# Splitting the softmax numerators into two tiles, each with its own DMA transposition

## The chip, the cores and the metric

The kernel runs on one core of a Trainium2 chip. The metric is the device time of one execution in microseconds. Beside it stands a profile of one execution, with the start and length of every instruction on every engine.

## The reference

Attention over pooled queries, then two feed-forward layers:

```python
q_pool = q.reshape(B, H, S // 2, 2, D).mean(axis=3)      # B 4, H 8, S 1152, D 64
scores = q_pool @ k.T / sqrt(D)                          # 576 x 1152 for each head
attn   = softmax(scores);  x = attn @ v                  # x: 2304 tokens x 512
h = x @ w_in;   x = (h * cos(h)) @ w_out                 # d_ff 2048
h = x @ w_in2;  out = (h * sigmoid(h)) @ w_out2
```

Everything is float32. The kernel gets near that accuracy with 16-bit matmuls: each operand is cut into a high half (rounded to float16) and a low half (the remainder, also float16), and the products high x high, low x high and high x low are summed.

## The kernel before

**Attention.** Heads are taken in 16 pairs (4 batches of 4). A pair gives 9 query tiles of 128 rows, 144 tiles in all. One tile goes through these steps:

- scores on TensorE (PE) into `sp`, line 391 (line 399 for the ninth tile of a pair, whose two halves belong to two heads);
- VectorE (DVE) scales them into `sc` and takes the maximum (line 410, two pieces; `nb` from line 415);
- ScalarE (ACT) makes the exponential in place (line 418), then writes the high numerators as float16 into the first half of `hl` (line 424, `tile_hi`);
- GpSimd (POOL) subtracts, which gives the low numerators in the second half of `hl` (line 429, `tile_lo`);
- one DMA transposition on SyncE's queue (SP, line 431) turns all of `hl`, 128 rows of 2304 numbers, into `hlT`, 18 blocks of 128 x 128;
- PE weighs V with it (`tile_pv`): for each of 9 blocks `c` a matmul with the high block against high and low V (130 columns, line 442) and one with the low block against high V (65 columns, line 446), into `pv`.

The tiles `sc`, `hl` and `hlT` have 4 buffers each. The weighing of a tile is written 4 tiles behind its scores (`LAG`).

**Around it.** Beside the attention of batches 1 to 3, PE, ACT, DVE and POOL work on the first feed-forward layer of finished batches (lines 522 to 594). Its input blocks `xn` take a buffer of `hl` and are transposed by line 508, 16 blocks of 128 x 128 in one DMA. The first layer's weights are decoded during batch 0 (lines 206 to 240), the second layer's during and after batch 3. The second layer comes last (PE lines 522 and 603).

**Order.** All DMAs of the kernel are issued by SP, in one queue: loads of q, k, v and weights (lines 177, 293 to 302), transpositions of q and k (`qT`, `kT`, lines 357 and 367, 18 blocks each) and of the numerators. The order on every engine is fixed when the program is built, by priorities and by the builder's own estimate of times; on the chip each engine runs its list strictly in that order.

Of the kernel before, what the change touches and what calls it, by code (L numbers as in the profile page):

```python
# [12 lines left out]
F16 = mybir.dt.float16  # L13
I32 = mybir.dt.int32
AF = mybir.ActivationFunctionType
ALU = mybir.AluOpType
# [11 lines left out]
NB_N, NB_SC, NB_H, NB_T, NB_S = 2, 4, 4, 4, 5  # L28
# [16 lines left out]
def attention_moe_moe_kernel(ctx, tc, q, k, v, w_in1, w_out1, w_in2, w_out2, out):  # L45
# [3 lines left out]
    nc = tc.nc  # L49
    B, H, S, D = q.shape  # L50
    SQ = S // 2
    DM, DFF = w_in1.shape
    NC = DM // 128
    NF = DFF // 128
    KC = S // 128
# [22 lines left out]
    def scale_steps(m, pool, res, top, wide=False):  # L78

        n = m.shape[1]
        if wide:
            w = small.tile([128, 1], F32, name="mw", tag="mw")
            wi, mi = w.bitcast(I32), m.bitcast(I32)
            nc.vector.tensor_scalar(
                out=wi, in0=mi, scalar1=3, scalar2=0x3F800000, op0=ALU.logical_shift_left, op1=ALU.bitwise_and
            )
            nc.vector.scalar_tensor_tensor(  # L90
                out=wi, in0=mi, scalar=1 << 30, in1=wi, op0=ALU.bitwise_and, op1=ALU.bitwise_or
            )
            m = w
        bc = pool.tile([128, 2, GW], F32, tag="h", name="bm")[:, 0, 0:4]
        nc.tensor.matmul(bc[:, 0:n], mean, m, start=True, stop=True)
        yield
        s, u = res
        nc.vector.tensor_scalar(
            out=u, in0=bc[:, 0:n], scalar1=TINY, scalar2=2.0**(9 - top), op0=ALU.max, op1=ALU.mult
        )  # L100

        nc.vector.tensor_scalar(
            out=s.bitcast(I32), in0=u.bitcast(I32), scalar1=EXP_MASK, scalar2=EXP_MASK,
            op0=ALU.bitwise_and, op1=ALU.bitwise_xor,
        )
        nc.vector.tensor_scalar(
            out=u.bitcast(I32), in0=u.bitcast(I32), scalar1=EXP_MASK, scalar2=None, op0=ALU.bitwise_and
        )

    def absmax(out_, in_, axis=AX.X):  # L110
        nc.vector.tensor_reduce(out=out_, in_=in_, axis=axis, op=ALU.max, apply_absolute_value=True)
# [9 lines left out]
    def early(g, n):  # L121
        while True:
            with ahead(n):
                r = next(g, END)
            if r is END:
                return
            yield r
# [139 lines left out]
    def att_pools(stack):  # L267
        at = Weights()
        at.p = stack.enter_context(tc.tile_pool(name="att", bufs=2, side="right", reuse_waits="tile"))
        at.src_stack = ExitStack()  # L270
        at.src = at.src_stack.enter_context(tc.tile_pool(name="src", bufs=2, side="right", reuse_waits="tile"))
        at.ps_s = stack.enter_context(tc.tile_pool(name="ps_s", bufs=1, space=PSUM, side="right"))
        at.ps_v = stack.enter_context(tc.tile_pool(name="ps_v", bufs=1, space=PSUM, side="right"))
        return at
# [103 lines left out]
    def tile_scores(at, P, t):  # L378


        T = Pair()
        T.P, T.t = P, t

        parts = [(0, 512), (512, S)]
        T.sp = [(a, z, at.ps_s.tile([128, z - a], F32, tag="sp%d" % a, name="sp")) for a, z in parts]
        if t < 2 * NT:
            kT = P.kT[t // NT]
            for a, z, sp in T.sp:
                for o, n in segs:
                    for e in range(2 if a <= o < z else 0):  # L390
                        nc.tensor.matmul(  # L391
                            sp[:, o - a:o - a + n], P.qT[e][:, t, :], kT[:, o:o + n], start=(e == 0), stop=(e == 1)
                        )
        else:
            for a, z, sp in T.sp:
                for o, n in segs:
                    for e in range(2 if a <= o < z else 0):
                        for i in range(2):
                            nc.tensor.matmul(
                                sp[i * 64:(i + 1) * 64, o - a:o - a + n], P.qT[e][:, t, i * 64:(i + 1) * 64],  # L400
                                P.kT[i][:, o:o + n], start=(e == 0), stop=(e == 1),
                            )
        return T
# [14 lines left out]
        nc.scalar.activation(out=T.sc, in_=T.sc, func=AF.Exp, scale=-1.0, bias=nb)  # L418

    def tile_hi(at, T, on_act):  # L420
        T.hl = at.p.tile([128, 2, S], F16, tag="hl", name="hl", bufs=NB_H)
        hi = T.hl[:, 0, :]
        if on_act:
            nc.scalar.activation(out=hi, in_=T.sc, func=AF.Copy)  # L424
        else:
            nc.vector.tensor_copy(hi, T.sc)

    def tile_lo(at, T):
        nc.gpsimd.tensor_tensor(out=T.hl[:, 1, :], in0=T.sc, in1=T.hl[:, 0, :], op=ALU.subtract)  # L429
        T.hlT = at.p.tile([128, 2, KC, 128], F16, tag="hlT", name="hlT", bufs=NB_T)  # L430
        nc.sync.dma_start_transpose(
            out=T.hlT.rearrange("p e c k -> p (e c) k"), in_=T.hl.rearrange("p e s -> p (e s)")
        )

    def tile_pv(at, T):
        P, t, G = T.P, T.t, T.G
        if T.gi == 0:
            G.pv = at.ps_v.tile([128, GT, 2, D + 1], F32, tag="pv", name="pv")
        hs = [(slice(0, 128), t // NT)] if t < 2 * NT else [(slice(0, 64), 0), (slice(64, 128), 1)]
        for r, i in hs:  # L440
            for c in range(KC):
                nc.tensor.matmul(  # L442
                    G.pv[r, T.gi], T.hlT[:, 0, c, r], P.vt[i][:, c],
                    start=(c == 0), stop=(c == KC - 1), skip_group_check=True,
                )
                nc.tensor.matmul(  # L446
                    G.pv[r, T.gi, 0], T.hlT[:, 1, c, r], P.vt[i][:, c, 0],
                    start=False, stop=(c == KC - 1), skip_group_check=True,
                )

# [25 lines left out]
    def x_scale_consts(w, s, u, first):  # L476


        c = Weights()
        uo = w.uoT if first else w.uo  # L480
        c.k = small.tile([128, 1], F32, tag="ck", name="ck", bufs=3)
        c.a = small.tile([128, w.npc], F32, tag="ca%d" % w.npc, name="ca", bufs=3)
        c.y = small.tile([128, uo.shape[1]], F32, tag="cy%d" % first, name="cy", bufs=3)
        two_pi = 2.0 * math.pi
        nc.vector.tensor_scalar(
            out=c.k, in0=s, scalar1=w.kg, scalar2=two_pi if first else 1.0, op0=ALU.mult, op1=ALU.mult
        )
        nc.vector.tensor_scalar(
            out=c.a, in0=w.ui, scalar1=u, scalar2=0.25 / two_pi if first else 0.25, op0=ALU.mult, op1=ALU.mult
        )  # L490
        nc.vector.tensor_scalar(out=c.y, in0=uo, scalar1=u, scalar2=w.ug, op0=ALU.mult, op1=ALU.mult)
        return c

    def x_split(at, mp, x32, i, blk, w):

        m = small.tile([128, 1], F32, name="xm", tag="xm")
        absmax(m, x32, AX.XY)
        yield
        s = small.tile([128, 1], F32, name="xs", tag="xs")
        u = small.tile([128, 1], F32, name="xu", tag="xu")  # L500
        yield from early(scale_steps(m, ps_h, (s, u), 14), P_CH)
        blk.c = x_scale_consts(w, s, u, True)
        xn = at.p.tile([128, 2, 2, DM], F16, tag="hl", name="xn", bufs=NB_H)
        nc.scalar.activation(out=xn[:, 0], in_=x32, func=AF.Copy, scale=s)
        nc.vector.scalar_tensor_tensor(out=xn[:, 1], in0=x32, scalar=s, in1=xn[:, 0], op0=ALU.mult, op1=ALU.subtract)
        yield
        blk.T = mp.p.tile([128, 2, 2, NC, 128], F16, tag="x%d" % i, name="xT", bufs=1)
        nc.sync.dma_start_transpose(
            out=blk.T.rearrange("p e t c k -> p (e t c) k"), in_=xn.rearrange("p e t d -> p (e t d)")
        )  # L510
        blk.xh = lambda c: blk.T[:, 0, :, c, :]
        blk.xl = lambda c: blk.T[:, 1, :, c, :]

# [106 lines left out]
    if True:  # L620
# [6 lines left out]
        at = att_pools(att_stack)  # L627
# [67 lines left out]
        P = {}  # L695
# [23 lines left out]
        x32 = {}  # L719
# [27 lines left out]
        def drain_pv():  # L747
            T = inflight.pop(0)
            G = T.G
            with ahead(P_PV):  # L750
                tile_pv(at, T)
# [35 lines left out]
        for n, (b, j) in enumerate(pairs):  # L787
# [7 lines left out]
            for o in range(0, len(seq), GT):  # L795
                G = Pair()
# [9 lines left out]
            for idx, (G, gi, t) in enumerate(order):  # L806
                with ahead(P_SC):
                    T = tile_scores(at, P[n], t)
# [40 lines left out]
        for i in range(2):  # L849
            T = wpool.tile([128, B, 2, 128], F16, tag="x32_%d" % i, name="xrT")  # L850
# [68 lines left out]
        for n in range(NB):  # L919
            nyb = y_load(n + 1) if n + 1 < NB else None  # L920
            gen = y_split(nyb) if nyb else None
            for f in range(NF):
# [7 lines left out]
                if len(pend) > 8:  # L930
                    blk, ff, nn = pend.pop(0)
# [43 lines left out]
```

## Time and profile before

| | |
|---|---|
| time, median of 3 runs | 1414.32 us (1410.59 to 1415.83) |
| profiled execution, first to last instruction | 1411.7 us |
| mean granted TensorE clock | 0.928 of full speed |
| busy: PE, DVE, ACT, POOL | 82%, 70%, 54%, 40% of the span |

The profiled execution's span of 1411.7 us is within the spread of the three timed runs, 2.6 us below their median; nothing else is recorded around it. The attention lasts from the start to about 860 us. From there to about 1008 us the rest of the first layer runs beside the decoding of the second layer's weights, and from 1008 us to the end the second layer, with PE all but always busy. The busy shares are averages over these stages, so each stage is read by itself.

### The profile page before, as it was taken

How to read it: one execution, taken by the hardware profiler on the slowest of the kernel's cores; microseconds unless marked ns; L12 is line 12 of the kernel's file. 1: busy time of each engine (PE TensorE's matmuls, PEld its weight loads, DVE VectorE, ACT ScalarE, POOL GpSimd, SP SyncE). 2: the span in 40 equal slices, each digit the busy share in tenths (PEclk: the TensorE clock that was granted, in tenths of full speed). 3: DMA queues.
4: the chain of work that ended last, by engine and by line, in shares of the span. 5: the costliest groups of instructions: out<-in, count | busy, mean ns of one | idle time of the engine just before them, and what ended most of it. 6: DMA issues, size and time to landing. Idle time of an engine off the chain costs nothing. (4 is left out here: it accounts for less than half of the span.)

```text
span 1411.7 us, 24909 instructions
## 1 busy us (share of the span) xinstructions
PE 1164.1 (82%) x10020; PEld 853.2 (60%) x10020; DVE 988.5 (70%) x1848; ACT 768.7 (54%) x907; POOL 568.2 (40%) x296
## 2 busy tenths in 40 slices
PE   1465356787897768898889889978899999999998
PEld 0243233475675556666667678867776666666664
DVE  7999997678678888977999985999933322223221
ACT  3686487668777678777788785555421111111110
POOL 1577276535656466646666563553600000000000
PEclk9966568799999899999999999989999999999999
DMA  7799789987799999989999964544110000000001
GB/s 232 190 238 213 186 157 206 202 167 137 149 194 171 198 205 205 176 156 185 156 208 182 220 131 86 147 120 129 52 60 31 31 6 25 31 31 16 16 2 29
DMA packets 493075, 186.17 MB, mean 132 GB/s; under 512 B 433056, under 2 KB 467872, under 8 KB 492960
## 3 DMA queue, kind: packets, MB, share of 16 engines
q1 hardware_dynamic: 492960, 184.59, 61.9%
q8 instruction: 78, 1.28, 0.4%
q14 instruction: 37, 0.30, 0.1%
HBM read 66.58 MB, written 9.44 MB: 54 GB/s over the span
## 5 line engine op out<-in xcount | busy, mean ns | idle before, releaser
L429 POOL TENSOR_TENSOR hl<-sc,hl 128x1152 f16<-128x1152 f32 x144 | 368.7, 2569 | 194.0 <-ACT hl L424 109.8
L391 PE MATMUL sp<-kT,qT 128*128 128x512 f16 (+1 forms) x768 | 196.2, 373 | 112.0 <-DVE sc L410 85.9
L535 ACT ACTIVATE hk<-h,ca 128x512 f32<-128x512 f32 x144 | 97.9, 682 | 318.0 <-PE h L522 318.0
L522 PEld LDWEIGHTS <-ih 128*128 128x128 f16 x2304 | 227.3, 100 | 66.9 <-issue 7.3
L410 DVE TENSOR_SCALAR_CACHE_REDUCE sc<-sp,psu 128x512 f32<-128x512 f32 (+1 forms) x288 | 229.0, 807 | 48.1 <-PE sp L391 46.8
L418 ACT ACTIVATE sc<-sc,nb 128x1152 f32<-128x1152 f32 x144 | 179.9, 1250 | 91.0 <-DVE nb L415 78.2
L442 PE MATMUL pv<-vt,hlT 128*128 128x130 f16 (+1 forms) x1440 | 196.1, 238 | 37.4 <-DMA hlT<-hl 29.6
L522 PE MATMUL h<-ys,ih 128*128 128x256 f16 x1152 | 196.2, 273 | 1.0 <-ACT hk L535 1.0
L522 PE MATMUL h<-xT,ih 128*128 128x256 f16 x1024 | 190.6, 280 | 2.1 <-ACT hk L535 1.3
L442 PEld LDWEIGHTS <-hlT 128*128 128x128 f16 (+1 forms) x1440 | 148.0, 111 | 67.3 <-DMA hlT<-hl 39.5
L446 PE MATMUL pv<-vt,hlT 128*128 128x65 f16 (+1 forms) x1440 | 188.4, 208 | 0.0
L391 PEld LDWEIGHTS <-qT 128*128 128x128 f16 x768 | 78.0, 110 | 180.0 <-issue 138.5
L424 ACT ACTIVATE hl<-sc 128x1152 f16<-128x1152 f32 x144 | 165.3, 1155 | 23.4 <-DMA hlT<-hl 12.2
L570 DVE TENSOR_SCALAR gh<-hk,ck 128x1024 f16<-128x1024 f32 x36 | 27.0, 751 | 206.2 <-PE o L603 198.6
L582 PE MATMUL y<-gl,oh 128*128 128x256 f16 x576 | 158.4, 275 | 2.9 <-POOL gl L563 2.9
L582 PE MATMUL y<-gh,oh 128*128 128x256 f16 x576 | 158.4, 275 | 2.1 <-ACT y L591 2.1
L582 PE MATMUL y<-gh,ol 128*128 128x256 f16 x576 | 158.4, 275 | 0.0
L522 PE MATMUL h<-ys,il 128*128 128x256 f16 x576 | 157.0, 273 | 0.0
L446 PEld LDWEIGHTS <-hlT 128*128 128x128 f16 (+1 forms) x1440 | 143.3, 108 | 15.9 <-issue 6.0
L522 PE MATMUL h<-xT,il 128*128 128x256 f16 x512 | 143.1, 280 | 0.0
L522 PEld LDWEIGHTS <-il 128*128 128x128 f16 x1152 | 114.4, 99 | 18.0 <-issue 1.3
L582 PEld LDWEIGHTS <-oh 128*128 128x128 f16 x1152 | 112.5, 99 | 20.1 <-issue 4.2
(283 smaller groups left out, 2024.5 us busy)
## 6 DMA issues: line engine op xcount, KB each, us to landing
wst<-in_moe_w_in_dram SPq DMA_DIRECT2D x16, 1024.0 KB, 5.9
wst<-in_moe_w_out_dram SPq DMA_DIRECT2D x16, 1024.0 KB, 5.9
stk<-in_k_dram SPq DMA_DIRECT2D x32, 288.0 KB, 4.3
stv<-in_v_dram SPq DMA_DIRECT2D x32, 288.0 KB, 4.4
stq<-in_q_dram SPq DMA_DIRECT2D x32, 256.0 KB, 3.1
ydr<-y SPq DMA_DIRECT2D x9, 512.0 KB, 2.9
y32b<-ydr SPq DMA_DIRECT2D x9, 512.0 KB, 3.2
out_dram<-osb SPq DMA_DIRECT2D x16, 256.0 KB, 2.1
```

Source lines behind the costliest of these rows:

```text
L391: nc.tensor.matmul(sp[:, o - a:o - a + n], P.qT[e][:, t, :], kT[:, o:o + n], start=(e == 0), stop=(e == 1))
L410: nc.vector.tensor_scalar(out=T.sc[:, a:z], in0=sp, scalar1=T.P.su, scalar2=None, op0=ALU.mult, op1=ALU.min, accum_out=mx[:, x:x + 1],)
L418: nc.scalar.activation(out=T.sc, in_=T.sc, func=AF.Exp, scale=-1.0, bias=nb)
L424: nc.scalar.activation(out=hi, in_=T.sc, func=AF.Copy)
L429: nc.gpsimd.tensor_tensor(out=T.hl[:, 1, :], in0=T.sc, in1=T.hl[:, 0, :], op=ALU.subtract)
L442: nc.tensor.matmul(G.pv[r, T.gi], T.hlT[:, 0, c, r], P.vt[i][:, c], start=(c == 0), stop=(c == KC - 1), skip_group_check=True,)
L446: nc.tensor.matmul(G.pv[r, T.gi, 0], T.hlT[:, 1, c, r], P.vt[i][:, c, 0], start=False, stop=(c == KC - 1), skip_group_check=True,)
L522: nc.tensor.matmul(hp, wt[:, c, f * 128:(f + 1) * 128], xt(c), start=(i == 0), stop=(i == 3 * NC - 1), skip_group_check=True,)
L535: nc.scalar.activation(out=o, in_=blk.hp, func=AF.Copy if first else AF.Silu, scale=blk.c.a[:, g:g + 1])
L570: nc.vector.tensor_scalar(out=gh, in0=hk, scalar1=blk.c.k, scalar2=None, op0=ALU.mult)
L582: nc.tensor.matmul(blk.y[:, oc, :], wt[:, f, oc * 128:(oc + 1) * 128], gt[:, f % 4, :], start=(f == 0 and e == 0 and oc % 2 == 0), stop=(f ...
```

## The change

`hl` becomes two tiles, `ehi` and `elo`, and `hlT` becomes `ehiT` and `eloT`, with 4 buffers each, so the memory stays the same. Each has its own DMA transposition of 9 blocks: that of `ehi` is issued after ACT's copy, that of `elo` after POOL's subtraction. In the weighing, the 9 matmuls with high blocks come first and the 9 with low blocks after them, where they alternated before. `xn` is cut in the same way, with two transpositions of 8 blocks.

```diff
     def tile_hi(at, T, on_act):
-        T.hl = at.p.tile([128, 2, S], F16, tag="hl", name="hl", bufs=NB_H)
-        hi = T.hl[:, 0, :]
+        T.hl = [at.p.tile([128, S], F16, tag=nm, name=nm, bufs=NB_H) for nm in ("ehi", "elo")]
+        T.hlT = [at.p.tile([128, KC, 128], F16, tag=nm, name=nm, bufs=NB_T) for nm in ("ehiT", "eloT")]
         if on_act:
-            nc.scalar.activation(out=hi, in_=T.sc, func=AF.Copy)
+            nc.scalar.activation(out=T.hl[0], in_=T.sc, func=AF.Copy)
         else:
-            nc.vector.tensor_copy(hi, T.sc)
+            nc.vector.tensor_copy(T.hl[0], T.sc)
+        nc.sync.dma_start_transpose(out=T.hlT[0], in_=T.hl[0])
 
     def tile_lo(at, T):
-        nc.gpsimd.tensor_tensor(out=T.hl[:, 1, :], in0=T.sc, in1=T.hl[:, 0, :], op=ALU.subtract)
-        T.hlT = at.p.tile([128, 2, KC, 128], F16, tag="hlT", name="hlT", bufs=NB_T)
-        nc.sync.dma_start_transpose(
-            out=T.hlT.rearrange("p e c k -> p (e c) k"), in_=T.hl.rearrange("p e s -> p (e s)")
-        )
+        nc.gpsimd.tensor_tensor(out=T.hl[1], in0=T.sc, in1=T.hl[0], op=ALU.subtract)
+        nc.sync.dma_start_transpose(out=T.hlT[1], in_=T.hl[1])
...
             for c in range(KC):
                 nc.tensor.matmul(
-                    G.pv[r, T.gi], T.hlT[:, 0, c, r], P.vt[i][:, c],
-                    start=(c == 0), stop=(c == KC - 1), skip_group_check=True,
+                    G.pv[r, T.gi], T.hlT[0][:, c, r], P.vt[i][:, c],
+                    start=(c == 0), stop=False, skip_group_check=True,
                 )
+            for c in range(KC):
                 nc.tensor.matmul(
-                    G.pv[r, T.gi, 0], T.hlT[:, 1, c, r], P.vt[i][:, c, 0],
+                    G.pv[r, T.gi, 0], T.hlT[1][:, c, r], P.vt[i][:, c, 0],
                     start=False, stop=(c == KC - 1), skip_group_check=True,
                 )
...
-        xn = at.p.tile([128, 2, 2, DM], F16, tag="hl", name="xn", bufs=NB_H)
-        nc.scalar.activation(out=xn[:, 0], in_=x32, func=AF.Copy, scale=s)
-        nc.vector.scalar_tensor_tensor(out=xn[:, 1], in0=x32, scalar=s, in1=xn[:, 0], op0=ALU.mult, op1=ALU.subtract)
+        xn = [at.p.tile([128, 2, DM], F16, tag=nm, name="xn", bufs=NB_H) for nm in ("ehi", "elo")]
+        nc.scalar.activation(out=xn[0], in_=x32, func=AF.Copy, scale=s)
+        nc.vector.scalar_tensor_tensor(out=xn[1], in0=x32, scalar=s, in1=xn[0], op0=ALU.mult, op1=ALU.subtract)
         yield
         blk.T = mp.p.tile([128, 2, 2, NC, 128], F16, tag="x%d" % i, name="xT", bufs=1)
-        nc.sync.dma_start_transpose(
-            out=blk.T.rearrange("p e t c k -> p (e t c) k"), in_=xn.rearrange("p e t d -> p (e t d)")
-        )
+        for e in range(2):
+            nc.sync.dma_start_transpose(
+                out=blk.T[:, e].rearrange("p t c k -> p (t c) k"), in_=xn[e].rearrange("p t d -> p (t d)")
+            )
```

On SP's queue, early in the second batch, behind the transposition of an input block, there stood before ("x6" is six equal rows in a run):

```order
L508 DMA_TRANSPOSE xT<-xn 128x16x128
L431 DMA_TRANSPOSE hlT<-hl 128x18x128 x6
L293 DMA stq<-in_q_dram 128x512
L357 DMA_TRANSPOSE qT<-qn 128x18x128
L431 DMA_TRANSPOSE hlT<-hl 128x18x128
L367 DMA_TRANSPOSE kT<-kn 128x18x128
```

Some rows further, around the same transpositions of q and k, there stands now:

```order
L302 DMA stk<-in_k_dram 128x576
L427 DMA_TRANSPOSE ehiT<-ehi 128x9x128
L431 DMA_TRANSPOSE eloT<-elo 128x9x128
L427 DMA_TRANSPOSE ehiT<-ehi 128x9x128
L431 DMA_TRANSPOSE eloT<-elo 128x9x128
L427 DMA_TRANSPOSE ehiT<-ehi 128x9x128
L431 DMA_TRANSPOSE eloT<-elo 128x9x128
L293 DMA stq<-in_q_dram 128x512
L357 DMA_TRANSPOSE qT<-qn 128x18x128
L427 DMA_TRANSPOSE ehiT<-ehi 128x9x128
L431 DMA_TRANSPOSE eloT<-elo 128x9x128
L367 DMA_TRANSPOSE kT<-kn 128x18x128
```

Each row of `hlT` has become two, a high one and a low one, nearly always next to each other; what stands between the tiles is as before.

On PE, at the weighing of the 72nd tile, there stood before (L391 is scores of a later tile):

```order
L391 LDWEIGHTS qT
L391 MATMUL sp<-kT,qT 128x512
L442 LDWEIGHTS hlT
L442 MATMUL pv<-vt,hlT 128x130
L446 LDWEIGHTS hlT
L446 MATMUL pv<-vt,hlT 128x65
L442 LDWEIGHTS hlT
L442 MATMUL pv<-vt,hlT 128x130
```

At the same tile there stands now, where its high matmuls end and its low ones begin:

```order
L440 LDWEIGHTS ehiT
L440 MATMUL pv<-vt,ehiT 128x130
L391 LDWEIGHTS qT
L391 MATMUL sp<-kT,qT 128x512
L391 LDWEIGHTS qT
L391 MATMUL sp<-kT,qT 128x512
L445 LDWEIGHTS eloT
L445 MATMUL pv<-vt,eloT 128x65
L445 LDWEIGHTS eloT
L445 MATMUL pv<-vt,eloT 128x65
```

The pairs of a high and a low matmul have come apart into two runs, and the builder has put other work between the runs, here two score matmuls; it does so in 102 of the 144 tiles.

## Rows read from the trace of the kernel before

**Rows 1.** Busy time of each engine by stage (columns: see below).

```profile
200.00:300.00 100.00, 71.21 (x694) 50.41 (x694) 75.51 (x180) 70.22 (x87) 52.01 (x32) 0.81 0.99 186
...
400.00:530.00 130.00, 99.71 (x1072) 75.63 (x1070) 106.43 (x234) 93.47 (x116) 75.84 (x47) 0.92 1.03 195
530.00:860.00 330.00, 292.34 (x2963) 223.72 (x2961) 283.62 (x544) 252.99 (x305) 195.90 (x99) 0.97 0.92 178
```

(The columns are the stretch, its length, busy time and instructions of PE, of PE's weight loads, of DVE, ACT and POOL, the granted clock, the DMA engines' share, and GB/s.)

**Rows 2.** Waits, whole span: engine and line, what for, total us, times, longest.

```profile
PEld L442 <- DMA hlT<-hl: 39.5, 27, 3.9
...
PE sp L391 <- DVE sc L410: 85.9, 63, 4.8
```

**Rows 3.** Tile `hlT`, 0 to 200 us: who waited for it (us, times).

```profile
  PEld L442: 6.1, 5
```

**Rows 4.** Tile `hlT`, 200 to 300 us: issue time (ns min/median/max), waits, landing.

```profile
L431 SPq DMA_TRANSPOSE hlT<-hl x19: 2543/3240/4172, 199.7 to 282.6; - x19
...
  PEld L442: 15.9, 12
```

**Rows 5.** Tile `hlT`, 400 to 530 us: the same.

```profile
L431 SPq DMA_TRANSPOSE hlT<-hl x26: 2683/3278/4442, 402.0 to 525.7; - x26
...
  PEld L442: 16.4, 9
...
DMA to landing us min/median/max: 4.6/5.5/6.9
```

**Rows 6.** Tile `hlT`, 530 to 860 us: who waited for it.

```profile
  PEld L442: 1.1, 1
```

**Rows 7.** Tile `hl`, whole span: subtraction, transposition (ns min/median/max), landing.

```profile
L429 POOL TENSOR_TENSOR hl<-sc,hl x144: 2356/2379/3388, 41.6 to 846.1; 128x1152 f16<-128x1152 f32 x144
L431 SPq DMA_TRANSPOSE hlT<-hl x144: 2436/2848/10194, 44.0 to 851.8; - x144
...
DMA to landing us min/median/max: 4.5/4.9/12.2
```

**Rows 8.** SP's own waits, 200 to 300 us.

```profile
SPq L431 <- POOL hl L429: 25.0, 10, 4.9
```

**Rows 9.** SP's own waits, 400 to 530 us.

```profile
SPq L431 <- POOL hl L429: 22.9, 12, 2.8
```

**Rows 10.** SP's queue in order of time, 436 to 503 us: start, us, what.

```profile
437.48 3.44 SPq L431 DMA_TRANSPOSE hlT<-hl  x1
...
450.33 12.24 SPq L431 DMA_TRANSPOSE hlT<-hl  x4
...
499.96 2.00 SPq L508 DMA_TRANSPOSE xT<-xn  x1
502.07 3.18 SPq L431 DMA_TRANSPOSE hlT<-hl  x1
```

**Rows 11.** Tile `xrT`, the transposition of 8 blocks: issue time and landing.

```profile
L851 SPq DMA_TRANSPOSE xrT<-xnr x2: 1232/1240/1247, 895.5 to 899.3; - x2
...
DMA to landing us min/median/max: 3.1/3.9/4.8
```

**Rows 12.** Tile `xT`, 855 to 872 us: two transpositions of 16 blocks.

```profile
L508 SPq DMA_TRANSPOSE xT<-xn x2: 1779/1820/1862, 862.5 to 868.7; - x2
```

**Rows 13.** PE in order of time at a weighing: start, us, what.

```profile
410.93 0.22 PE L442 MATMUL pv<-vt,hlT 128*128 128x130 f16 x1
410.98 0.19 PE L446 MATMUL pv<-vt,hlT 128*128 128x65 f16 x1
411.01 0.22 PE L442 MATMUL pv<-vt,hlT 128*128 128x130 f16 x1
```

**Rows 14.** SP's own waits, whole span.

```profile
SPq L431 <- POOL hl L429: 163.3, 68, 10.3
...
SPq L431 <- PE pv L446: 53.8, 23, 8.2
```

**Rows 15.** PE's waits, 200 to 300 us: for the transposed k.

```profile
PE sp L391 <- DMA kT<-kn: 9.3, 2, 4.7
```

## The prediction

> **What bounds the kernel now.** First the busy time by stage [rows 1]. No engine is full while the attention runs: from 200 to 300 us PE is busy 71.2 of 100 us and DVE 75.5, from 400 to 530 us PE 99.7 of 130 and DVE 106.4. In the long stage from 530 to 860 us PE comes to 292.3 of 330 us, 89%. The change touches only the attention, so the question is what PE waits for there. The view of the waits, over the whole span, names two candidates [rows 2]: the weighing waits 39.5 us, in 27 pieces, for the transposed numerators, and the scores wait 85.9 us for DVE to empty `sp`. The change can act on the first alone.
>
> The same wait by stage says where it lies: 6.1 us before 200 us [rows 3], 15.9 us from 200 to 300 us [rows 4], 16.4 us from 400 to 530 us [rows 5], and 1.1 us from 530 to 860 us [rows 6]. These make 39.5 us. In the last stage numerators lie ready when PE comes to them. Two stretches of 230 us hold 32.3 us of the wait in 21 pieces, and only there can much be won.
>
> Next, why numerators are late there. POOL's subtraction takes 2.38 us, the issue of the transposition 2.85 us on SP, and it lands 4.9 us after its issue began [rows 7]. In the two stretches SP is close to full: 19 issues at a median of 3.24 us are 62 of 100 us [rows 4], 26 at 3.28 us are 85 of 130 us [rows 5], and q, k, `xn` and loads come on top. From 437 to 502 us it issues without a pause [rows 10]. Yet in the same stretches SP also stands still for the subtraction, 25.0 us in 10 pieces [rows 8] and 22.9 us in 12 [rows 9]: a burst of tiles finds a queue that idled just before. So there the bound is SP's queue of transpositions, and behind it PE.
>
> **The change part by part.** *The high half goes out early.* SP's 22 waits for the subtraction average 47.9/22 = 2.2 us. Now the high half can be issued in that time. What 9 blocks cost to issue no row shows. Between 8 blocks at 1.24 us [rows 11] and 16 at 1.82 us [rows 12] a block adds 0.0725 us, so 9 would take 1.31 us. Between 8 blocks and the shortest issue of 18, 2.44 us [rows 7], it adds 0.12 us and 9 take 1.36 us. With 1.31 us the 22 waits take in 29 us of issue that lies behind them today.
>
> *Two issues in place of one.* Two halves are 2.62 to 2.72 us, against 2.44 us at the shortest and 2.85 us at the median for a whole [rows 7], with some 0.1 us between two issues (the last one in [rows 10] ended at 501.96 us and the run went on at 502.07 us). A tile thus costs SP between 0.13 us less and 0.38 us more. I take 0.1 us more, near the middle: for the 45 tiles of the two stretches 4.5 us. Net, SP gains about 25 us of 230 us. In the other stages the extra issue lies under the slack that the 1.1 us of waiting shows [rows 6]. The part of a transfer that follows its issue, 4.9 - 2.85 = 2.05 us, lies under the next issue already: four in a row take 12.24 us, 3.06 us each [rows 10], although each lands 5.5 us after its start [rows 5].
>
> The Trainium skill speaks against the split: DMA: Bandwidth & Descriptors, section Rules for kernel authors, tells to join small transfers into large ones, and its section on the anatomy of a DMA gives about 2.0 us fixed and bytes over 436 GB/s (fitted for the path that GpSimd issues). By that, as an estimate, a whole of 590 KB would take 3.35 us and a half 2.68 us, so 2.0 us more a tile if the fixed part stood in the queue, 90 us of SP for the 45 tiles. The trace agrees that there are some 2 us besides the issue, and differs in that they do not hold up the next transfer.
>
> *The weighing starts with the high half.* A high and the next low matmul start 0.05 us apart, a low and the next high one 0.03 us [rows 13]; so the nine high ones are 9 x 0.05 = about 0.5 us, and they now run while the low half is on its way. Over 27 waits that is 13.5 us. Together with the shorter queue I expect the wait for numerators to fall from 39.5 to about 15 us, 24 us less (bounds: 13.5 us if SP gains nothing, 39.5 us if all goes).
>
> *What is late next.* PE will meet the next wait sooner. From 530 to 860 us, where numerators are never late, PE still idles 37.7 us of 330 [rows 1], and scores that wait for DVE are the largest wait of the kernel [rows 2]. DVE with 75% to 82% in the two stretches [rows 1] cannot follow at once. I take half of the 24 us: 12 us.
>
> *The runs of matmuls.* Nine low matmuls in a run need a new block of weights every 0.03 us, where the alternation needs one every 0.04 us on average. The row of 0.03 us [rows 13] shows that one such step is possible, not nine. Bounds: nothing, or 9 x 0.01 = 0.1 us a tile, 14 us of PE in all 144 tiles if weights come no faster than in the alternation. I take 2 us on the path, because PE has the idle time named above. High blocks in a run need them every 0.05 us, which is slower than now.
>
> *The input blocks.* Eight transpositions of 16 blocks become 16 of 8: 2 x 1.24 = 2.48 us in place of 1.82 us [rows 11, 12], 0.7 us each on SP, in part while the low half is still being made. Two of them fall in the crowded stretches: 1 us.
>
> *The order.* The builder has put other work between the two runs in 102 of 144 tiles, which is what lets PE go on when the low half is late; the rest of the order moves little.
>
> The sum is -12 + 2 + 1 = -9 us. Against the profiled 1411.7 us that is 1402.7 us; the median of the timed runs lies 2.6 us above the profile, so **1405 us**, 0.65% less. About 0.5%, 7 us, is what a measurement of this kernel can tell from no change.
>
> **The rivals.** *The gain is eaten by the next wait.* PE then waits for DVE's emptying of `sp` by as much as it saved on numerators. For it speaks that DVE is busier than PE in both stretches [rows 1] and that this wait is twice as large [rows 2]; against it, that the crowded queue is SP's, which is relieved. Then the gain is 0 to 4 us: about 1412 us, no change.
>
> *A half costs SP more than half.* SP wins 29/45 = 0.65 us a tile from the early start, so it breaks even at (2.85 + 0.65 - 0.1)/2 = 1.7 us a half. At 2.0 us a half, 45 tiles cost 45 x (4.1 - 2.85) = 56 us more less 29 us, 27 us of SP, and with half of it reaching PE, 13 us: 1427 us. For it speaks that two blocks more than 16 cost 0.66 us at the shortest (2.44 against 1.78 us, [rows 7, 12]), so that some counts might be dear; against it the 1.24 us of 8 blocks [rows 11]. The Trainium skill's rule of joining transfers, above, is this rival in its harshest form.
>
> *The low blocks are kept longer.* The low run now stands behind other PE work in 102 tiles, so `eloT` comes free later, and SP already waits 53.8 us in 23 pieces for PE to free `hlT` [rows 14]. Everything in SP's queue stands behind that wait, transposed k among it, for which PE lost 9.3 us from 200 to 300 us [rows 15]. If each of the 23 waits grows by 1 us, SP loses 23 us, mostly after 530 us where there is slack; it decides from the point where this is more than the 9 us of gain, and with half on the path the time is 1414.3 - 9 + 12 = 1417 us, with a share of late k up to 1424 us.
>
> **How the numbers follow.** My forecast has 0.44, the eaten gain 0.34, dear halves 0.12, low blocks kept longer 0.10. The likeliest gives 1405 us. The low end takes the 24 us with nothing late next and no cost: 1390 us, and I put it at 1392. The high end takes in the third rival's 1424 us and leaves out most of the second. So 1392 to 1424 us; the forecast's own range is 1397 to 1410 us (half of the bounds 39.5 and 13.5 us gained, less the 3 us of costs). Faster by over 0.5%: 0.44. Within: 0.34. Slower: 0.22.
>
> **What would show it.** Right: the wait of the weighing for `ehiT` and `eloT` together near 15 us and mostly on `eloT`; issues of 9 blocks at 1.3 to 1.4 us; SP's waits for POOL shorter; landing of a half near 3 to 4 us. Wrong: issues near 2 us (second rival), SP waiting longer for PE (third), or shorter waits for numerators with the wait of scores for DVE longer by as much (first). I would also be wrong if the stage before 200 us, where I count nothing, moved by more than a few us.

## The result and the profile after

| | before | after |
|---|---|---|
| time, median of 6 runs each | 1412.41 us (1410.59 to 1415.83) | 1424.69 us (1418.67 to 1427.20) |
| ratio, 95% interval | | 1.0083 [1.0062, 1.0104] |
| profiled execution, first to last instruction | 1411.7 us | 1424.8 us |

The change costs 0.83%. Forecast were 0.65% less and a range that ended at 1424 us, so both the direction and, by 0.7 us, the range were missed.

The page of the changed kernel, busy time by engine:

```profile
PE 1170.7 (82%) x10020; PEld 854.9 (60%) x10020; DVE 1019.5 (72%) x1848; ACT 766.2 (54%) x905; POOL 569.0 (40%) x296
```

Its busy time by stage (columns as in [rows 1]):

```profile
200.00:300.00 100.00, 65.49 (x639) 44.29 (x638) 76.92 (x180) 71.04 (x86) 55.02 (x32) 0.83 1.01 181
...
400.00:530.00 130.00, 98.98 (x1034) 73.54 (x1031) 109.01 (x225) 92.80 (x113) 75.54 (x43) 0.90 1.02 188
530.00:860.00 330.00, 289.50 (x2889) 219.98 (x2887) 295.44 (x552) 257.46 (x309) 195.43 (x102) 0.97 0.94 178
```

Against [rows 1] two things stand out. From 200 to 300 us PE started 639 matmuls where it had started 694. And from 530 to 860 us DVE is busy 295.4 us in place of 283.6 with nearly the same number of instructions (552 and 544), while PE did less.

The transpositions and the subtraction (ns min/median/max), and the landing of `ehiT`:

```profile
L427 SPq DMA_TRANSPOSE ehiT<-ehi x144: 1242/1325/4677, 41.9 to 863.0; - x144
...
L430 POOL TENSOR_TENSOR elo<-sc,ehi x144: 2358/2378/3418, 41.9 to 859.9; 128x1152 f16<-128x1152 f32 x144
...
DMA to landing us min/median/max: 3.2/3.5/7.4
```

Nine blocks take 1.325 us to issue and land after 3.5 us: the term of 1.31 us was right, and the second rival (a half at 1.7 us or more) is out. SP's own waits:

```profile
SPq L431 <- POOL elo L430: 48.6, 45, 4.2
SPq L427 <- PE pv L440: 42.6, 18, 5.6
SPq L427 <- ACT ehi L424: 38.0, 33, 4.0
...
SPq L431 <- PE pv L445: 11.0, 8, 2.6
```

SP waits 48.6 us for POOL where it waited 163.3 [rows 14]. That too came as forecast. The next link did not. The waits of PE over the whole span:

```profile
PE sp L391 <- DVE sc L410: 83.1, 67, 9.4
...
PEld L440 <- DMA ehiT<-ehi: 29.0, 19, 4.2
...
PEld L445 <- DMA eloT<-elo: 17.7, 15, 4.2
```

The weighing waits 29.0 + 17.7 = 46.7 us for numerators, more than the 39.5 us of [rows 2], though SP's queue was relieved. The wait of the scores for DVE is as long as before (83.1 and 85.9 us), so the first rival, in which the one wait takes over from the other, is not what happened either.

### The profile page after: what moved, and what is told of

Read it like the earlier page. It is cut to its first block, busy times and chain, and to the rows that moved or that the text cites. A ratio compares the mean times of both kernels' runs of the same rounds, so it can differ in the third digit from the quotient of the medians.

```text
span 1424.8 us, 25187 instructions
## 1 busy us (share of the span) xinstructions
PE 1170.7 (82%) x10020; PEld 854.9 (60%) x10020; DVE 1019.5 (72%) x1848; ACT 766.2 (54%) x905; POOL 569.0 (40%) x296
## 4 chain that ended last, share of the span: by engine, by line
PE 42%; DVE 34%; issue 9%; ACT 7%; DMA 4%; POOL 1%; SPq 1%; DVEq 0%; ACTq 0%; POOLq 0%
PE h L522 16%; PE o L603 13%; DVE sc L410 7%; PE y L582 5%; PE sp L391 3%; DVE wst L215 3%; DVE tt L548 2%; PE pv L440 2%; DVE tt L557 2%; DVE wt L207 2%; DVE wst L218 2%; DVE pm L111 2%; DVE kn L311 2%; DVE vt L311 2%; DVE tt L547 2%
## 5 line engine op out<-in xcount | busy, mean ns | idle before, releaser
L430 POOL TENSOR_TENSOR elo<-sc,ehi 128x1152 f16<-128x1152 f32 x144 | 369.3, 2574 | 248.4 <-ACT ehi L424 162.1
L391 PE MATMUL sp<-kT,qT 128*128 128x512 f16 (+1 forms) x768 | 190.0, 368 | 98.1 <-DVE sc L410 83.1
L410 DVE TENSOR_SCALAR_CACHE_REDUCE sc<-sp,psu 128x512 f32<-128x512 f32 (+1 forms) x288 | 229.1, 807 | 43.3 <-PE sp L391 30.3
L440 PE MATMUL pv<-vt,ehiT 128*128 128x130 f16 (+1 forms) x1440 | 148.5, 238 | 40.4 <-DMA ehiT<-ehi 21.7
L391 PEld LDWEIGHTS <-qT 128*128 128x128 f16 x768 | 77.6, 107 | 167.4 <-issue 128.2
L424 ACT ACTIVATE ehi<-sc 128x1152 f16<-128x1152 f32 x144 | 164.9, 1155 | 6.2 <-DMA ehiT<-ehi 3.5
L440 PEld LDWEIGHTS <-ehiT 128*128 128x128 f16 (+1 forms) x1440 | 109.3, 109 | 67.0 <-DMA ehiT<-ehi 29.0
L563 POOL TENSOR_TENSOR gl<-tt,gh 128x1024 f16<-128x1024 f32 x36 | 90.8, 2522 | 75.8 <-DVE gh L562 75.2
L445 PE MATMUL pv<-vt,eloT 128*128 128x65 f16 (+1 forms) x1440 | 107.7, 202 | 13.5 <-DMA eloT<-elo 13.5
```

Of the source, the lines that this page charges most:

```text
L391: nc.tensor.matmul(sp[:, o - a:o - a + n], P.qT[e][:, t, :], kT[:, o:o + n], start=(e == 0), stop=(e == 1))
L410: nc.vector.tensor_scalar(out=T.sc[:, a:z], in0=sp, scalar1=T.P.su, scalar2=None, op0=ALU.mult, op1=ALU.min, accum_out=mx[:, x:x + 1],)
L424: nc.scalar.activation(out=T.hl[0], in_=T.sc, func=AF.Copy)
L430: nc.gpsimd.tensor_tensor(out=T.hl[1], in0=T.sc, in1=T.hl[0], op=ALU.subtract)
L440: nc.tensor.matmul(G.pv[r, T.gi], T.hlT[0][:, c, r], P.vt[i][:, c], start=(c == 0), stop=False, skip_group_check=True,)
L445: nc.tensor.matmul(G.pv[r, T.gi, 0], T.hlT[1][:, c, r], P.vt[i][:, c, 0], start=False, stop=(c == KC - 1), skip_group_check=True,)
```

## The experiments

All were timed against the kernel before in the same session; its median there lay between 1412.3 and 1414.3 us. Ratios stand with their 95% interval. One theory is used throughout: **the order**. The builder lays out every engine's list anew from priorities and its own estimate of times, so a change of two DMAs shifts work on all engines. The expectations have DVE's busy time move along with the time. Its first rival is **the queue**: two issues a tile cost, whatever the order.

### Parts of the change

Only the runs of matmuls, nine high and then nine low, in the kernel before:

```diff
-                    start=(c == 0), stop=(c == KC - 1), skip_group_check=True,
+                    start=(c == 0), stop=False, skip_group_check=True,
                 )
+            for c in range(KC):
```

> The kernel before, with one change: the nine high matmuls of a tile come first and the nine low ones after them; one tile hl and one transposition stay. Order theory (the 12 us come from the newly built order, by which instructions of DVE fall beside POOL's subtractions and are held up, not from any single part of the change): a time anywhere from 1405 to 1425 us, DVE's busy time moving with it. Theory of the matmul runs (the low run holds PE and the buffers): 1420 to 1427 us, like the full change. Queue theory (two issues for one cost SP): 1412 us, like before.

1415.66 us, ratio 1.0016 [0.9996, 1.0035], with DVE busy 990.8 us. The runs, in an order built anew here too, cost nothing that can be measured. In the changed kernel's trace a run of six low matmuls reads (start, us, what):

```profile
642.97 0.34 PE L445 MATMUL pv<-vt,eloT 128*128 128x65 f16 x6
```

One of them lasts 0.19 us, so six begin (0.34 - 0.19)/5 = 0.03 us apart: the single step of [rows 13] can be kept up.

The split without the runs (the changed kernel with the second `for c` taken out):

> The changed kernel with high and low matmuls alternating again, so two tiles and two transpositions, but the old order of the weighing. Queue theory: 1420 to 1427 us. Theory of the matmul runs: 1412 us or less. Order theory: anywhere from 1405 to 1425 us, DVE's busy time (1020 us in the changed kernel, 989 before) moving with it.

1422.17 us, 1.0066 [1.0042, 1.0090], with DVE busy 999.5 us. This order was built anew, so either theory can still read it.

The split with both transpositions written behind the subtraction, which was to take the early start away:

```diff
-        nc.sync.dma_start_transpose(out=T.hlT[0], in_=T.hl[0])
...
-        nc.sync.dma_start_transpose(out=T.hlT[1], in_=T.hl[1])
+        for e in range(2):
+            nc.sync.dma_start_transpose(out=T.hlT[e], in_=T.hl[e])
```

> The changed kernel with both halves issued after the subtraction, so two transpositions but no early start. If the early start were worth the 10 us or so that was forecast and another cost hid it, this is slower than the changed kernel by that, 1430 us or more. Queue theory: 1424 us or more. Order theory: anywhere from 1405 to 1425 us.

1424.73 us, 1.0092 [1.0066, 1.0118]: the same as the whole change. But the edit did not take the early start away. In the two traces every engine has the same operations in the same order, SP's transpositions included, and the high one begins before its tile's subtraction has ended in 43 tiles here and in 44 in the changed kernel. So this is the changed kernel timed once more (DVE busy 1015.0 us, against 1019.5), and what the early start is worth by itself was not measured. Split numerators beside an unsplit `xn` were not tried.

The kernel before with one priority shifted, nothing else:

```diff
-P_CH, P_SC, P_EX, P_PV, P_MS, P_MU, P_W, P_PR, P_X = 0, 60, 0, -100, 200, 0, 0, 0, 0
+P_CH, P_SC, P_EX, P_PV, P_MS, P_MU, P_W, P_PR, P_X = 0, 58, 0, -100, 200, 0, 0, 0, 0
```

> The kernel before with one number of the builder changed, the priority of the score matmuls (58 in place of 60): the same instructions in another order on every engine. Order theory: it differs from 1412 us by something like the 12 us in question, either way, and DVE's busy time goes along. Both other theories: 1412 us within 4 us.

1430.78 us, 1.0131 [1.0103, 1.0159]: the same instructions in another order cost more than the whole change does. DVE's busy time did not go along: it is 988.5 us, as before.

### Order and instructions exchanged

To part the two, the order of every engine was written down and fixed (`ORDER` holds, for each engine, the places of its instructions; each is tied to the one ahead of it without a semaphore):

```diff
         attention_moe_moe_kernel(tc, *args)
+        pinned(nc, tc)
...
+        for a, b in zip(at, at[1:]):
+            tc.add_manual_dep(
+                mine[b], mine[a].name,
+                mybir.DependencyInfo(mybir.DependencyClass.NoSync, mybir.DependencyReason.DATA),
+                reason="order",
+            )
```

The control:

> The kernel before, with the order in which each engine issues its instructions written down and fixed as it was: a control for the next two runs. Every theory expects the time of the kernel before in this comparison, within 0.3% (about 1412 us). If it differs, fixing an order costs something of its own and the next two runs must be read against this one.

1413.06 us, 0.9991 [0.9974, 1.0008]. Fixing an order costs nothing.

> The whole change (two tiles, two transpositions a tile, nine high and then nine low matmuls, the split of xn), but every engine issues in the order of the kernel before: on VectorE, ScalarE, GpSimd and TensorE the same operations at the same places, the eighteen matmuls of a head exchanged among their own places, and on SP the two transpositions at the place of the one. Order theory (the loss comes from the order that was newly built): 1410 to 1416 us, ratio 1.000 +- 0.003. Theory of the two issues on SP (they cost, in whatever order): 1422 to 1427 us, ratio 1.007 to 1.010. Together with the run after it the two theories are told apart crosswise.

**1410.26 us, 0.9977 [0.9959, 0.9995].** The whole change, in the order of before, costs nothing and is at most a little faster. Its waits for numerators, and above them that of the scores for DVE:

```profile
PE sp L391 <- DVE sc L410: 88.9, 64, 4.9
...
PEld L440 <- DMA ehiT<-ehi: 18.0, 13, 3.0
...
PEld L445 <- DMA eloT<-elo: 10.6, 16, 1.7
```

The waits for numerators are 28.6 us, against 39.5 before and 46.7 in the changed kernel. So the weighing does wait less, as forecast, by 11 us, and some 2 us of time are left of it.

> The opposite: nothing of the split (one numerator tile, one transposition of 18 blocks at the place of the low one, xn whole; only the nine-then-nine order of the matmuls, which cost nothing alone), but every engine issues in the order that was built for the changed kernel. Order theory: slow like the changed kernel, 1421 to 1427 us, ratio 1.006 to 1.010, with VectorE's busy time at about 1015 us or more. Theory of the two issues on SP: 1410 to 1416 us.

**1450.41 us, 1.0247 [1.0219, 1.0276].** With the split undone the new order is not fast but slower still, further than either theory had it. Its wait for numerators:

```profile
PEld L442 <- DMA hlT<-hl: 101.8, 41, 8.9
```

In this order the split is worth some 25 us (1450.4 against 1424.7), probably because this order puts the weighing where the halves are due and a whole is not. The crosswise result refutes the queue theory: the instructions of the change are neutral or better in both orders, and the new order costs 14 us with them, known to some 4 us.

> The changed kernel with the priority of the score work at 58 instead of 60, the same small shift of the order that made the kernel before 16 us slower. Order theory: an order is a draw, so the time may go either way by up to 16 us from the changed kernel's 1425 and need not follow the shift of the kernel before; any change beyond 0.5% speaks for it. Theory of the two issues on SP: the reordering costs what it cost before, about +16 us, giving 1440 us.

1421.01 us, 1.0053 [1.0037, 1.0068], 3.7 us (0.3%) below the changed kernel. The shift that cost 16 us there costs nothing here. That speaks against the queue theory's 1440 us, but stays short of the 0.5% that the order theory had named.

### Where in the program the order costs

From here on every run has the changed kernel's instructions; only the order differs by stretch, cut at the first weighing of tile 24 (about 220 us) and of tile 132 (about 780 us).

> The changed kernel's instructions in both cases from here on; only the order differs. Here every engine follows the newly built order until the first weighing of numerator tile 24 (about 220 us), then the order of before. Start theory (the 11 us by which the changed kernel is late at tile 24 are what it ends late by): slow, 1421 to 1427 us. Tail theory (the loss is made after about tile 132, where VectorE binds): 1410 to 1414 us, the lateness at tile 24 being made up again as it was by tile 130 in the changed kernel.

> The opposite: the order of before until the first weighing of tile 24, then the newly built one. Start theory: 1410 to 1414 us. Tail theory: 1421 to 1427 us.

> The order of before until the first weighing of tile 132 (about 780 us), then the newly built one; six more weight decoding operations of VectorE then lie ahead of the cut than in the newly built order. Tail theory in the form that the order of the last stretch costs: 1419 to 1427 us. Tail theory in the form that the decoding left over for the last stretch costs: 1410 to 1414 us, as for the start theory.

> The newly built order until the first weighing of tile 132, then the order of before, with six decoding operations more left for the last stretch than before had there. Order of the last stretch costs: 1410 to 1414 us. Decoding left over costs: 1420 to 1427 us. Start theory: 1421 to 1427 us.

> The changed kernel's instructions; the newly built order only between the first weighings of tiles 24 and 132, the order of before ahead of it and behind it. If the loss is a sum of what each stretch loses (from the four runs before: about 5 us to tile 24, 6 us between, 3 to 4 us behind tile 132): 1414 to 1418 us. If it needs the newly built start as well, so that it stays near the whole change in the old order: 1409 to 1412 us.

> The complement: the order of before only between tiles 24 and 132, the newly built one ahead of it and behind it. Sum of the stretches: 1417 to 1421 us. If the middle alone decides: 1410 to 1413 us.

What they measured, each expectation in its own row (in the order above: rows 2, 6, 4, 5, 3 and 7):

| order to tile 24 / to 132 / to the end | us | ratio to before | sum of the parts |
|---|---|---|---|
| old / old / old | 1410.26 | 0.9977 [0.9959, 0.9995] | |
| new / old / old | 1415.56 | 1.0018 [0.9996, 1.0040] | +5.3 |
| old / new / old | 1415.57 | 1.0021 [1.0006, 1.0036] | +5.3 |
| old / old / new | 1414.16 | 1.0005 [0.9985, 1.0025] | +3.9 |
| new / new / old | 1421.98 | 1.0063 [1.0039, 1.0087] | 1420.9 |
| old / new / new | 1420.02 | 1.0042 [1.0020, 1.0065] | 1419.5 |
| new / old / new | 1419.93 | 1.0054 [1.0035, 1.0073] | 1419.5 |
| new / new / new (the change) | 1424.69 | 1.0083 [1.0062, 1.0104] | 1424.8 |

The three single stretches, added to 1410.3 us, give each of the other four within 1.1 us. So neither the start theory nor the tail theory holds alone: the loss is spread over the program, about 5, 5 and 4 us, each known to 3 to 4 us, so that an agreement within 1.1 us is in part luck. The form of the tail theory that lays the loss on leftover decoding comes close in rows 4 and 5 (at most 1414 and at least 1420 us forecast), but rows 2 and 6 lie between the theories. The sum of the stretches, drawn from the first four of these runs, forecast the last two rightly.

### By what means it costs

In the changed kernel DVE is busy 1019.5 us, in the same instructions in the old order 991.5:

```profile
PE 1166.9 (83%) x10020; PEld 855.3 (61%) x10020; DVE 991.5 (70%) x1848; ACT 768.2 (54%) x907; POOL 568.8 (40%) x296
```

How the 28 us more come about is seen in the order of time, DVE of the changed kernel (start, us, what):

```profile
836.91 2.86 DVE L210 TENSOR_SCALAR wt<-wt 128x1024 int32<-128x1024 int32 x1
...
839.75 3.08 DVE L548 SCALAR_TENSOR_TENSOR tt<-tt,hk 128x1024 f32<-128x1024 f32 x1
...
854.10 3.40 DVE L548 SCALAR_TENSOR_TENSOR tt<-tt,hk 128x1024 f32<-128x1024 f32 x1
...
888.51 1.23 DVE L548 SCALAR_TENSOR_TENSOR tt<-tt,hk 128x1024 f32<-128x1024 f32 x1
```

and POOL in the same time:

```profile
836.45 2.77 POOL L430 TENSOR_TENSOR elo<-sc,ehi 128x1152 f16<-128x1152 f32 x1 [1.48 <-ACT ehi L424]
839.18 2.57 POOL L563 TENSOR_TENSOR gl<-tt,gh 128x1024 f16<-128x1024 f32 x1
...
854.05 2.38 POOL L430 TENSOR_TENSOR elo<-sc,ehi 128x1152 f16<-128x1152 f32 x1 [0.54 <-DVE tt L547]
```

At 888.51 us L548 takes 1.23 us. At 854.10 us, begun 0.05 us behind a subtraction that ended at 854.05 + 2.38 = 856.43 us, it takes 3.40 us and ends at 857.50, 1.07 us after POOL. L210 and L548 at 837 and 840 us likewise end 0.55 and 1.08 us after POOL's operation. Such an operation of DVE stands still until POOL is done; which ones are hit depends on the order. That fits a rule of the Trainium skill, SBUF — State Buffer, section SBUF: two separate sides: DVE and GpSimd share one pair of ports to SBUF under an exclusive lock, and a DVE operation with two SBUF inputs or in a two-port mode blocks for the whole of a GpSimd instruction that was first. The trace agrees in the times above, and in the operation that reads its data from PSUM, which is the same in both orders, here the changed kernel (mean 807 ns, 807 ns in the old order too, and 809 ns in the run below in the new order with the subtraction cut down):

```profile
L410 DVE TENSOR_SCALAR_CACHE_REDUCE sc<-sp,psu 128x512 f32<-128x512 f32 (+1 forms) x288 | 229.1, 807 | 43.3 <-PE sp L391 30.3 <-POOL elo L430 6.6 <-PE sp L399 3.2
```

Over the whole trace of the changed kernel, L548 takes 2.30 us on average in the 29 places where it overlaps an operation of POOL by over 0.2 us, and 1.22 us in the 7 others. L207, which works on SBUF too, is not held: 1.21 us in its 18 places beside POOL and in its 14 others. All that DVE's operations take above the shortest of their kind comes to 245 us in the changed kernel and to 216 us in the old order. Of the 29 us between, 21.5 lie in operations whose longest overlap is with a subtraction, 7 in those beside another operation of POOL, and under 1 in those beside none. That accounts for DVE's 28 us; it does not say yet what they cost in time.

Two runs take the subtraction away (the part of the computation that their expectations name), in either order:

```diff
-        nc.gpsimd.tensor_tensor(out=T.hl[1], in0=T.sc, in1=T.hl[0], op=ALU.subtract)
-        nc.sync.dma_start_transpose(out=T.hlT[1], in_=T.hl[1])
+        nc.gpsimd.tensor_tensor(out=T.hl[1][:, :16], in0=T.sc[:, :16], in1=T.hl[0][:, :16], op=ALU.subtract)
+        nc.sync.dma_start_transpose(out=T.hlT[1], in_=T.hl[0])
```

> The changed kernel in the newly built order, but GpSimd's subtraction of a tile covers 16 of its 1152 columns, and the low transposition reads the high tile, so nothing waits for GpSimd: that part of the computation is left out. Theory that VectorE's 31 us of additional busy time come from lying beside GpSimd's subtraction: VectorE's busy time falls from 1019 us to that of the next run, within 5 us, and the distance between the two runs falls to under 5 us. Rival, that the order's waits and not the stretched operations cost: the distance stays at 10 to 15 us.

> The same cut of GpSimd's subtraction in the changed kernel's instructions issued in the order of before: what the run before is read against. Both theories: at or below 1410 us; VectorE's busy time falls below 991 us, to 950 us or less if operations beside the subtraction are stretched as the traces suggest.

1370.18 us, 0.9699 [0.9676, 0.9723], and 1370.61 us, 0.9704 [0.9681, 0.9728]: the distance of the two orders is gone. The page's busy line, first of the new order, then of the old:

```profile
PE 1158.1 (85%) x10020; PEld 850.7 (62%) x10020; DVE 883.2 (65%) x1848; ACT 764.5 (56%) x905; POOL 243.9 (18%) x296
```

```profile
PE 1155.8 (84%) x10020; PEld 845.9 (62%) x10020; DVE 874.0 (64%) x1848; ACT 767.7 (56%) x907; POOL 242.4 (18%) x296
```

DVE is busy 136 and 118 us less, with the same instructions. Nine of the 28 us of difference stay (forecast: under 5). Counted as above, they lie in operations beside POOL's other work, 75.2 us over the shortest in the new order and 65.2 in the old.

These two runs took away two things, POOL's time and the wait of the low transposition for it. The last pair keeps the whole subtraction and takes only that wait away:

```diff
         nc.gpsimd.tensor_tensor(out=T.hl[1], in0=T.sc, in1=T.hl[0], op=ALU.subtract)
-        nc.sync.dma_start_transpose(out=T.hlT[1], in_=T.hl[1])
+        nc.sync.dma_start_transpose(out=T.hlT[1], in_=T.hl[0])
```

> The changed kernel in the newly built order, GpSimd's subtraction at its full 1152 columns, but the low transposition reads the high tile, so that nothing waits for the subtraction: the low half is left out of the result. It separates what the two runs before took away together. Stretching theory (VectorE beside the subtraction): VectorE's busy time stays at 1010 us or more and the distance to the next run stays at 8 to 15 us. Waiting theory (the low transposition queues on SP behind a subtraction that the order puts late): the distance falls to under 4 us although VectorE is as busy as in the changed kernel.

> The same unread subtraction in the order of before, which the run before is read against. Stretching theory: VectorE busy near 990 us and 8 to 15 us faster than the run before. Waiting theory: within 4 us of the run before. Both: 1400 to 1412 us.

1423.22 us, 1.0081 [1.0059, 1.0104], and 1411.61 us, 0.9992 [0.9977, 1.0007]: the distance is back, 11.6 us, and the difference of DVE's busy time with it. New order and old:

```profile
PE 1171.7 (82%) x10020; PEld 855.1 (60%) x10020; DVE 1013.5 (71%) x1848; ACT 766.1 (54%) x905; POOL 566.9 (40%) x296
```

```profile
PE 1172.0 (83%) x10020; PEld 858.9 (61%) x10020; DVE 986.9 (70%) x1848; ACT 768.0 (54%) x907; POOL 568.8 (40%) x296
```

So the waiting theory, as its expectation puts it, falls: the order's cost needs the subtraction on POOL, not the wait of the low transposition for it. But one thing still waits for the subtraction in these two runs, though their expectations say that nothing does. The subtraction reads `sc`, and DVE cannot write the next scores into that buffer before it has ended. New order:

```profile
DVE sc L410 <- POOL elo L430: 8.7, 3, 3.2
```

In the old order of this pair no such wait is recorded; in the changed kernel it is 6.6 us, with its instructions in the old order 2.4. No run parts this rival from the stretching of DVE. So that it is the stretching, and not this wait, POOL's time itself or the slack that 42 us less leave everywhere, is not shown. Two more results limit it. The kernel before with the shifted priority lost 16 us with DVE as busy as before:

```profile
PE 1174.6 (82%) x10020; PEld 856.5 (60%) x10020; DVE 988.5 (69%) x1848; ACT 769.4 (54%) x907; POOL 565.5 (40%) x296
```

And old/new/new with 1017.0 us of DVE takes as long as new/old/new with 994.5. It is thus not DVE's total that sets the time. Either it counts where a stretched operation stands, or orders lose by other waits; how much of the 14 us is which stays open.

In the profiles the two orders part at the end of the attention. First the changed kernel, then the same instructions in the old order (columns as in [rows 1]):

```profile
823.00:860.00 37.00, 28.40 (x284) 22.42 (x281) 33.04 (x54) 26.60 (x35) 15.41 (x7) 0.91 0.61 119
```

```profile
823.00:860.00 37.00, 34.80 (x406) 29.15 (x405) 27.16 (x54) 25.30 (x34) 20.98 (x8) 1.00 0.67 135
```

As many DVE instructions take 33.0 in place of 27.2 us, and PE starts 284 matmuls in place of 406. Both kernels make the numerators of the 137th tile at the same time (ACT's copy starts at 808.6 and 808.7 us), and those of the last, the 144th, 14.4 us apart (858.6 and 844.2 us). Most of this is not the subtraction's doing: with it cut to 16 columns these seven tiles still take 43.7 us in the new order and 32.1 in the old, 11.5 us more, where with it they take 50.0 and 35.5, 14.5 us more. Without it the new order is 15 us ahead at the 137th tile (755.1 and 770.4 us), and so is no later in spite of them. The granted clock is 0.91 and 1.00 in this stretch, but its mean over the whole execution is 0.927 in both, so it does not make the 14 us. In the changed kernel the decoding has fallen behind as well; from 823 to 1055 us, in the changed kernel and in the old order:

```profile
L548 DVE SCALAR_TENSOR_TENSOR tt<-tt,hk 128x1024 f32<-128x1024 f32 x14 | 27.8, 1986 | 0.1
L215 DVE SCALAR_TENSOR_TENSOR wst<-wst,wt 128x1024 int32<-128x1024 int32 x15 | 27.5, 1832 | 0.1
```

```profile
L548 DVE SCALAR_TENSOR_TENSOR tt<-tt,hk 128x1024 f32<-128x1024 f32 x14 | 19.0, 1358 | 0.1
...
L215 DVE SCALAR_TENSOR_TENSOR wst<-wst,wt 128x1024 int32<-128x1024 int32 x13 | 15.8, 1217 | 0.0
```

15 steps of decoding are left in place of 13, and one of L215 takes 1.83 us in place of 1.22. Other lines go the other way (L547 11.9 us in place of 18.6, L557 26.1 in place of 29.9); DVE as a whole is busy 193.5 us there in place of 186.0. PE's first matmul of the second layer's output (L603) starts at 1053.8 us in the changed kernel and at 1040.3 us in the old order; the ends lie as far apart (1424.8 and 1411.4 us), so all of the loss is made before it.

## Why the prediction was wrong

**The step that failed** is the last one of the sum, that of the order: "the rest of the order moves little". It was costed at nothing, and it is worth +14 us (1424.7 against 1410.3 us with the same instructions). The order had been read for where the two halves stand on SP and for the runs on PE; that SP's list looks alike there says nothing about where DVE's, ACT's and POOL's operations now stand. No term of the sum was for an order in which these engines do the same work later. What the runs do not show is by which means the order costs. The count beside that step is off too: in the changed kernel's trace other work stands between the last high and the first low matmul in only about a quarter of the tiles. Some 100 tiles have other work anywhere among their 18 matmuls, which 102 seems to count.

**Two issues, 1.31 us each:** right, 1.325 us. **SP's waits for the subtraction:** fell, as forecast. **The runs of matmuls, +2 us:** nothing to be measured (1.0016 [0.9996, 1.0035]), and the step of 0.03 us is kept up.

**The wait for numerators, 39.5 to 15 us:** right in direction in the old order, too large. There it fell to 28.6 us, 11 us in place of 24, and of the forecast gain of 9 us some 2 us remained (0.9977 [0.9959, 0.9995]). The fall counted every wait of SP for the subtraction as issue time won. But with the change in the old order SP waits for ACT instead, in front of the high transposition, where the kernel before has no wait for ACT at L431 at all:

```profile
SPq L431 <- POOL elo L430: 40.7, 41, 2.5
...
SPq L427 <- ACT sc L418: 29.4, 24, 4.5
SPq L427 <- ACT ehi L424: 27.4, 23, 6.1
```

And the transposition of the high half begins before its tile's subtraction has ended in only 30 of the 144 tiles (44 in the changed kernel). In the newly built order, which moves the weighing as well, the wait did not fall at all.

**The rivals.** The eaten gain gives the time of the run in the old order (1410 us, no change), but hardly its mechanism: the scores wait 88.9 us for DVE there against 85.9, 3 us more where 11 were saved. (That wait is the largest that PE has for another engine, not the largest of the kernel.) Dear halves are refuted by the issue time. Low blocks kept longer: SP waits 11.0 us for the low run in the changed kernel, 53.6 us for the two runs together, as long as the 53.8 us of [rows 14], so this is not the loss. No rival named the order.

**The stage before 200 us**, named as a place where the prediction could break, did break: 22 tiles have their high numerators by then in the changed kernel, 24 in the old order. By itself the order up to tile 24 costs some 5 us.

## What to carry to other kernels

Where a builder lays out all engines' lists, a small edit is two changes: what it does, and a new draw of the order, which here was worth 14 us against 2. Fix the old order, or exchange the orders, before crediting or blaming the edit; here the changed instructions in the old order, at 1410.3 us, are the best version found, though only just ahead of the kernel before. Then see that the edit changed what it was meant to change: a call moved in the text left every list here as it was. When a new order is judged, compare the mean of each DVE line in both traces: those that were held beside POOL here (L548, L215, L210) grow or shrink with the order, while L207 and L410 do not.

## What the runs showed of the hardware

One DVE operation of 128 x 1024 that takes 1.23 us takes 3.40 us when a POOL subtraction began 0.05 us ahead of it. It works the other way too: at 898.20 us a POOL operation (L563, 2.13 us at its shortest near there) takes 2.98 us behind an L548 that DVE began at 897.98 us. Cutting POOL's subtraction from 1152 to 16 columns took 118 to 136 us off the busy time of DVE, which had not been edited. Not every operation of DVE is held: L207 on SBUF takes 1.21 us beside POOL and away from it, and L410, which reads PSUM, 807 ns in both orders.
